# A gated unit whose normalisation and split go batch by batch, in a program whose order comes from another scheduling simulation

## The chip, the cores and the metric

The kernel runs on one core of one Trainium2 chip. The metric is the device time of one execution in microseconds. Five engines have instruction queues of their own: PE (TensorE, matmuls), DVE (VectorE), ACT (ScalarE), POOL (GpSimd) and SP (SyncE, which here issues the DMAs). Each works through its own queue in order, and semaphores tie the queues together; the order inside each queue is fixed when the program is built.

## The reference, cut to what matters

```python
def _attn_ref(q, k, v):                 # each (8, 8, 1152, 64): batch, head, position, head_dim
    q_pool = q.reshape(B, H, S // 2, 2, D).mean(axis=3)          # 576 queries
    scores = np.matmul(q_pool, k.transpose(0, 1, 3, 2)) / np.sqrt(D)
    attn = np.exp(scores - scores.max(-1, keepdims=True))
    attn = attn / (attn.sum(-1, keepdims=True) + 1e-09)
    return np.matmul(attn, v)

def _moe_ref(x, w_in, w_spatial, b_spatial, w_out):   # x: (8, 576, 512)
    h = np.maximum(x @ w_in, 0.0)                      # 512 -> 1024
    u, v = h[..., :512], h[..., 512:]
    mu, var = mean and variance of v over its 512 columns
    v_n = (v - mu) / np.sqrt(var + 1e-06)
    v_s = np.einsum('ts,bsd->btd', w_spatial, v_n) + b_spatial[None, :, None]
    return (u * v_s) @ w_out                           # 512 -> 512
```

So there are 8 batches of 8 heads of attention, and for each batch a gated unit: a projection, a normalisation of its second half over the columns, a mixing over the 576 positions, a gate and a second projection.

## The kernel before, in words

**Attention.** The heads go two at a time, so there are 32 pairs. For pair i, `attention` runs 18 steps (9 blocks of 128 keys, two heads). A step multiplies keys by queries in two matmuls of 512 columns (L506 and L507, float16 high part and low part) into a PSUM bank `pss` (three of them), and ACT takes the exponential (L512). After every second step POOL subtracts the high part of the result from the whole (`split`, L524), which yields the two operands of the multiplication with the values (L428, L432, L435, twelve short matmuls for a step). The last 64 queries of each head are kept apart (L520, L478 to L480). Beside pair i runs `maxima(i + 1)`: 27 products of queries and keys (L342, L333), each reduced on DVE to row maxima (L348) that a transposition (L356, one for each pair) and a DMA bring to where the next pair's scores need them. `prep` brings the keys and queries two pairs ahead, `values_ahead` the values. When a pair's values are complete, `turn_main` transposes them (L457) into `xg`, the gated unit's input.

**Weights.** The weights lie in memory as doubles. `load_weights` reads them in pieces of 128 x 512 and `from_double` (L144) turns each into float32 with six DVE instructions and two on ACT. Twelve pieces: eight of `w_in`, four of `w_out`. This is done beside pairs 0 to 8.

**Gated unit.** Two batches make a unit of 1,152 rows, so there are four units, `gated_unit(0)` to `gated_unit(3)`; unit n can begin when pair 8n + 7 is transposed. Units 0, 1 and 2 run beside the attention of the following pairs, unit 3 has nothing beside it but the end of pair 31. The 1,152 rows are nine tiles of 128: four of the first batch, one (tile 4) that holds the last 64 rows of both, four of the second. A unit has four stages:

1. the second half of the projection, nine tiles of twelve matmuls (L582), with relu (L590) and the statistics of each row (L592, L593). When all nine are done, the reciprocal square roots are made for all nine tiles at once by four Newton steps on DVE (L602 to L614);
2. the first half of the projection, transposed (L646, L656), twelve pieces. After each of the first nine, `normalise(t)` (L616) makes one tile's float16 high and low parts: two DVE instructions of 512 columns (L618, L624) and one on ACT (L623);
3. `spatial(e, fc)`, eight calls: the mixing over positions (L688, L689), the bias and the gate on DVE (L695, L698), the sum of squares on ACT (L700);
4. `split(0)` (L703), which finds one scale for the unit from all eight sums of squares, and makes the high and low parts of the gated values with eight instructions on ACT (L718) and eight on DVE (L719), then nine tiles of twelve matmuls (L731, `products`), a scaled copy and the store.

For the last unit, stage 4 is made in two groups of two column blocks: the first group's products are kept and the second group's are added (L773).

**What sets the order.** Every part is a Python generator, and a `yield` marks where another part may come in. The main loop (L809) steps the attention of a pair and with each step its neighbours at fixed rates; a unit gets one step for every two of the attention (`MOE_RATE`). The program order that results is only a priority: when the program is built, a scheduler runs it on a simulated machine, lets each simulated engine take the ready instruction of the highest priority, and writes down the order in which they were taken. That is each engine's queue. The machine simulated is that of the default scheduler (`TileContext(nc)`, L879).

## Time and profile before

| | us |
|---|---|
| median of 3 runs (lowest, highest) | 1373.64 (1370.13, 1375.04) |
| the profiled execution | 1378.83 |
| its span, first to last instruction | 1377.1 |

| engine | busy us | share of the span | instructions |
|---|---|---|---|
| PE | 1222.1 | 89% | 13,696 matmuls |
| DVE | 967.1 | 70% | 2,068 |
| ACT | 970.6 | 70% | 1,632 |
| POOL | 847.0 | 62% | 492 |

The profile's page gives sums over the whole program; the program has stages with different neighbours. What an engine does in a stretch is read from the view of windows (busy microseconds of each engine between two times, with the number of instructions in brackets and the granted TensorE clock), one instruction after another from the timeline. A matmul's duration overlaps that of the next, so PE's busy time says when PE had anything in flight, and not how much more it could have taken; for that the distance from one matmul's start to the next is to be read.

### The profile page before, as it was taken

The page shows a single profiled execution, that of the slowest core. Times are in us where ns is not written, and L with a number is a line of the kernel's source. Part 1 is how long each engine was busy: PE and PEld are TensorE (multiplying, and loading weights), DVE is VectorE, ACT ScalarE, POOL GpSimd, SP SyncE. Part 2 cuts the span into 40 slices and gives each one's busy share as a digit, 9 for nine tenths or more (in the row PEclk, how much of TensorE's full clock was granted, in tenths as well). Part 3 has the DMA queues.
Part 4 walks back from the last instruction along what each step waited for, and adds up shares of the span by engine and source line. Part 5 has one row for each costly group of instructions (what it writes and reads, how often), then busy time and mean ns, then how long its engine had stood idle before and what let it go on. Part 6 is the DMA issues. An engine that isn't in the chain of part 4 may idle for free.

```text
span 1377.1 us, 33478 instructions
## 1 busy us (share of the span) xinstructions
PE 1222.1 (89%) x13696; PEld 741.5 (54%) x13696; DVE 967.1 (70%) x2068; ACT 970.6 (70%) x1632; POOL 847.0 (62%) x492
## 2 busy tenths in 40 slices
PE   3677887788998999889998999889998999899998
PEld 1354555555554665556555666555555566556443
DVE  5799889986869767765668766775667866761455
ACT  6777678779966777768776886768776776655333
POOL 3587677878755666657774766667666576655000
PEclk9998899989999999999999999999999999999999
DMA  7533343434333231244332132244331131101002
GB/s 252 166 97 109 94 124 94 128 93 139 113 96 96 79 94 56 62 126 135 96 96 87 51 91 84 74 118 135 104 96 42 47 94 55 28 24 40 8 1 69
DMA packets 56346, 123.77 MB, mean 90 GB/s; under 512 B 8256, under 2 KB 16448, under 8 KB 56192
## 3 DMA queue, kind: packets, MB, share of 16 engines
q1 hardware_dynamic: 56192, 121.63, 29.8%
q8 instruction: 107, 1.75, 0.5%
q14 instruction: 47, 0.39, 0.1%
HBM read 83.56 MB, written 9.44 MB: 68 GB/s over the span
## 4 chain that ended last, share of the span: by engine, by line
PE 47%; DVE 25%; ACT 8%; POOL 7%; DMA 7%; issue 4%; SPq 1%; POOLq 0%; ACTq 0%; DVEq 0%
DVE mt L348 7%; PE pss L507 5%; PE pss L506 5%; PE pw L688 5%; POOL pt L524 4%; PE pm L342 4%; PE pw L731 4%; PE pw L646 3%; PE o L435 3%; PE o L428 3%; PE pw L582 3%; ACT pt L512 3%; DMA kq<-in_qT_dram 3%; PE o L432 3%; DVE vv L138 2%
## 5 line engine op out<-in xcount | busy, mean ns | idle before, releaser
L524 POOL TENSOR_TENSOR pt<-pt 128x1024 f16<-128x1024 f32 x288 | 567.8, 1977 | 265.9 <-ACT pt L512 253.8
L512 ACT ACTIVATE pt<-pss,lnp,esc 128x512 f32<-128x512 f32 x576 | 439.4, 776 | 156.7 <-PE pss L507 148.1
L348 DVE TENSOR_REDUCE mt<-pm 128x1 f32<-128x384 f32 x730 | 395.8, 552 | 139.1 <-PE pm L342 119.2
L435 PE MATMUL o<-vp,pt 128*128 128x65 f16 x2304 | 282.8, 198 | 20.2 <-POOL pt L524 19.9
L428 PE MATMUL o<-vp,pt 128*128 128x65 f16 x2304 | 284.8, 196 | 13.0 <-DVE xm L443 12.8
L506 PE MATMUL pss<-qhi,khi 128*128 128x64 f16 (+1 forms) x1152 | 279.6, 294 | 9.1 <-ACT pt L512 8.0
L432 PE MATMUL o<-vp,pt 128*128 128x64 f16 x2304 | 284.5, 196 | 0.0
L507 PE MATMUL pss<-xq,klo 66*128 66x64 f16 (+1 forms) x1152 | 280.6, 295 | 4.1 <-DMA xq<-mr 4.1
L428 PEld LDWEIGHTS <-pt 128*128 128x128 bf16 x2304 | 222.7, 101 | 85.1 <-DVE xm L443 22.0
L432 PEld LDWEIGHTS <-pt 128*128 128x128 bf16 x2304 | 221.6, 100 | 50.7 <-issue 10.5
L342 PE MATMUL pm<-khi,qhi 128*128 128x384 f16 x652 | 217.9, 335 | 32.6 <-DVE mt L348 27.7
L435 PEld LDWEIGHTS <-pt 128*128 128x128 f16 x2304 | 220.7, 100 | 31.6 <-POOL pt L524 24.8
L507 PEld LDWEIGHTS <-klo 66*128 66x128 f16 x1152 | 99.1, 100 | 48.8 <-issue 17.3
L132 ACT ACTIVATE klo<-kq 128x1152 f16<-128x1152 f32 x64 | 74.6, 1166 | 63.7 <-DMA kq<-in_kT_dram 49.4
L506 PEld LDWEIGHTS <-khi 128*128 128x128 f16 x1152 | 103.5, 100 | 27.9 <-issue 12.2
L342 PEld LDWEIGHTS <-qhi 128*128 128x128 f16 x768 | 76.8, 101 | 66.3 <-issue 28.5
L524 POOL TENSOR_TENSOR ptl<-ptl 128x1152 f16<-128x1152 f32 x32 | 71.1, 2221 | 57.9 <-ACT ptl L520 57.9
L305 POOL TENSOR_TENSOR klo<-kq,khi 128x640 f16<-128x640 f32 x64 | 85.1, 1341 | 20.1 <-ACT khi L304 19.8
L520 ACT ACTIVATE ptl<-pss,lnp,esc 128x256 f32<-128x256 f32 (+1 forms) x128 | 75.6, 591 | 24.8 <-PE pss L507 24.2
L264 POOL TENSOR_TENSOR vp<-vt,vp 128x576 f16<-128x576 f32 x64 | 80.6, 1264 | 20.3 <-ACT vp L262 20.3
L582 PE MATMUL pw<-wi_h,xg 128*128 128x512 f16 x240 | 90.1, 382 | 0.0
L731 PE MATMUL pw<-wo_h,vv 128*128 128x512 f16 x216 | 80.3, 381 | 4.7 <-DVE vv L138 4.7
(177 smaller groups left out, 2394.2 us busy)
## 6 DMA issues: line engine op xcount, KB each, us to landing
vt<-in_v_dram SPq DMA_DIRECT2D x64, 576.0 KB
kq<-in_kT_dram SPq DMA_DIRECT2D x32, 576.0 KB
kq<-in_qT_dram SPq DMA_DIRECT2D x32, 576.0 KB
khi<-khi SPq DMA_DIRECT2D x96, 144.0 KB
out_dram<-row SPq DMA_DIRECT2D x24, 256.0 KB
qhi<-xq SPq DMA_DIRECT2D x64, 72.0 KB
klo<-klo SPq DMA_DIRECT2D x32, 144.0 KB
vv<-in_w_in_dram SPq DMA_DIRECT2D x8, 512.0 KB
```

The source lines that it names most:

```text
L305: nc.gpsimd.tensor_sub(KL[:, 0, a:z], k0[:, a:z], khh[:, 1, a:z])
L342: nc.tensor.matmul(pm[:, :W], lhsT=qhl[:, h, c0 : c0 + P], rhs=khh[:, h, n * NB : (n + 1) * NB, :], start=True, stop=True,)
L348: nc.vector.reduce_max(out=mt[:, t, n : n + 1], in_=pm[:, :W], axis=AX.X)
L428: nc.tensor.matmul(o[:, t], lhsT=top[:, cols], rhs=vp[:, D : D + D1], start=c == 0 and t == 0, stop=False, skip_group_check=True,)
L432: nc.tensor.matmul(o[:, t, 0:D], lhsT=top[:, cols], rhs=vp[:, 0:D], start=False, stop=False, skip_group_check=True)
L435: nc.tensor.matmul(o[:, t], lhsT=rst[:, cols], rhs=vp[:, D : D + D1], start=False, stop=c == NC - 1, skip_group_check=True,)
L506: nc.tensor.matmul(o, lhsT=khh[:, h, c, :], rhs=qhl[:, h, q], start=True, stop=False)
L507: nc.tensor.matmul(o, lhsT=KL[0:KR, h, c, :], rhs=X[0:KR, h, q], start=False, stop=True)
L512: nc.scalar.activation(pt, ps, AF.Exp, bias=lnp, scale=esc)
L524: nc.gpsimd.tensor_sub(t.bitcast(F16)[:, :, 0::2], t, t.bitcast(BF16)[:, :, 1::2])
L582: nc.tensor.matmul(ph, lhsT=xa[:, cc, c0 : c0 + P], rhs=wa[:, cc, DH:DF], start=n == 0, stop=n == 3 * NCC - 1,)
L731: nc.tensor.matmul(py, lhsT=ga[:, fc, c0 : c0 + P], rhs=wa[:, fc, :], start=m == 0, stop=m == end - 1)
```

## The change

There are three edits. Line numbers in the changed program differ a little: L582 is now L626, L646 is L660, L688 and L689 are L702 and L703, L731 is L749.

1. `from_double` takes the low word as an unsigned number straight from the source, so the shift that made it signed (L151) is gone: five DVE instructions for a piece instead of six.
2. `gated_unit` works by batch. The reciprocal square roots are made twice, for tiles 0 to 4 after tile 4 and for tiles 5 to 8 after tile 8, with three Newton steps instead of four. `normalise` begins in stage 1, after tile 5, and goes on in stage 2 after every second piece. There is one scale for each batch instead of one for each unit (or group): `split(0)` runs beside the spatial stage of the second batch, `split(1)` and `split_tails` beside the products of the first batch's tiles. The parts are written over the normalised tiles that are no longer needed. All four units now go the same way; the last unit's two groups and their final addition are gone.
3. The context is made with `schedule_with_timeline_sim=True`: the scheduler's simulated machine is another one, so the order of every engine's queue is written anew.

```diff
-        V.tensor_scalar(out=t2, in0=lo, scalar1=1, scalar2=None, op0=ALU.logical_shift_right)
-        yield
-        V.scalar_tensor_tensor(out=dst, in0=t2, scalar=2.0 ** -51, in1=dst, op0=ALU.mult, op1=ALU.add)
+        yield
+        V.scalar_tensor_tensor(out=dst, in0=lo, scalar=2.0 ** -52, in1=dst, op0=ALU.mult, op1=ALU.add)
...
+        def deviations(c):
+            v_, s_, r_ = va[:, c], sd[:, c], rs[:, c]
+            nc.vector.tensor_scalar_add(v_, mv[:, c, 1], 1e-6)
...
+            for k in range(3):
+                z = SVN if k == 2 else 1.0
+                nc.vector.tensor_mul(s_, r_, r_)
...
+            if t > 4:
+                normalise(done)
+                done += 1
+            if t in (4, NT - 1):
+                deviations(slice(0, 5) if t == 4 else slice(5, NT))
+            yield
...
-                if done < NT:
+                if done < NT and (3 * fc + i) % 2 == 0:
                     normalise(done)
                     done += 1
...
+        def split(e):
+            s_g, r_g = yield from scale_of(gsq[:, e * NFC : (e + 1) * NFC], "g")
+            s_gs.append(s_g)
+            nc.vector.tensor_mul(r_y[:, e : e + 1], r_g, wsc["wo"])
...
+            m0 = 0 if e == 0 else MAIN + P
+            for fc in range(NFC):
+                x = u[:, fc, m0 : m0 + MAIN]
+                h, l = vh[:, 5 * e + fc, 0:MAIN], vh[:, 5 * e + fc, MAIN : 2 * MAIN]
+                head(h, x, s_g)
+                rest(l, x, s_g, h)
+                yield
+
+        def split_tails():
+            for e in range(2):
+                x = u[:, :, MAIN + e * TAIL : MAIN + (e + 1) * TAIL]
+                head(gte[:, 0, :, e], x, s_gs[e])
+                rest(gte[:, 1, :, e], x, s_gs[e], gte[:, 0, :, e])
+                yield
...
+        def chain(gens):
+            for g in gens:
+                yield from g
+
+        def beside(main, other, every):
+            for n, _ in enumerate(main):
+                if n % every == 0:
+                    other = step(other)
+                yield
+            while other is not None:
+                other = step(other)
+                yield
+
+        yield from chain(spatial(0, fc) for fc in range(NFC))
+        yield from beside(chain(spatial(1, fc) for fc in range(NFC)), split(0), 3)
+        yield from beside(chain(products(t) for t in range(4)), chain([split(1), split_tails()]), 2)
+        yield from chain(products(t) for t in (5, 6, 7, 8, 4))
...
-    with _tile.TileContext(nc) as tc:
+    with _tile.TileContext(nc, schedule_with_timeline_sim=True) as tc:
```

The order changes on every engine and all through the program. Three places show how.

**DVE, after the first pair's maxima.** (`mx`, `mr`, `qks`, `qkr`, `esc` and `qhi` belong to the chain from one pair to the next; `vv` and `u` at L149 to L161 are the pieces of the weights.) Before:

```order
L352 TENSOR_REDUCE mx<-mt 128x9
L149 TENSOR_SCALAR vv<-vv 128x512
L358 TENSOR_SCALAR mr<-pm 9x128
L117 TENSOR_SCALAR qkh<-pm 128x2
L359 SCALAR_TENSOR_TENSOR mr<-pm,mr 9x128
L121 TENSOR_SCALAR qks<-qkh 128x2
L122 TENSOR_SCALAR qkr<-qkh 128x2
L161 TENSOR_TENSOR u<-u,vv 128x512
L287 SCALAR_TENSOR_TENSOR esc<-qkr 128x1
L151 TENSOR_SCALAR vv<-vv 128x512
L138 SCALAR_TENSOR_TENSOR qhi_120<-kq,qks,xq_114 128x576
```

The same place now (L139 is the former L138, L118 to L123 the former L117 to L122):

```order
L352 TENSOR_REDUCE mx<-mt 128x9
L358 TENSOR_SCALAR mr<-pm 9x128
L118 TENSOR_SCALAR qkh<-pm 128x2
L359 SCALAR_TENSOR_TENSOR mr<-pm,mr 9x128
L122 TENSOR_SCALAR qks<-qkh 128x2
L123 TENSOR_SCALAR qkr<-qkh 128x2
L287 SCALAR_TENSOR_TENSOR esc<-qkr 128x1
L159 SCALAR_TENSOR_TENSOR vv<-vv 128x512
L150 TENSOR_SCALAR vv<-vv 128x512
L139 SCALAR_TENSOR_TENSOR qhi_120<-kq,qks,xq_114 128x576
```

The short chain instructions no longer have a piece of the weights between them, but more pieces have gone through by then: of the instructions at L149 to L161, 10 of 72 stood ahead of the 27th maximum and 22 ahead of the 54th; now 15 of 60 and 36.

**PE, unit 1's products.** Before, beside pairs 22 to 24, three matmuls of the unit (L731) stand between two steps of the attention:

```order
L506 LDWEIGHTS khi_118
L506 MATMUL pss<-qhi_121,khi_118 128x512
L507 LDWEIGHTS klo_109
L507 MATMUL pss<-xq_115,klo_109 128x512
L342 LDWEIGHTS qhi_119
L342 MATMUL pm<-khi_116,qhi_119 128x384
L731 LDWEIGHTS vv
L731 MATMUL pw<-wo_h,vv 128x512
L731 LDWEIGHTS vv
L731 MATMUL pw<-wo_l,vv 128x512
L731 LDWEIGHTS vv
L731 MATMUL pw<-wo_h,vv 128x512
```

Now the first products of unit 1 (L749) come in a run, behind a run of attention:

```order
L507 LDWEIGHTS klo_107
L507 MATMUL pss<-xq_113,klo_107 128x64
L749 LDWEIGHTS vv
L749 MATMUL pw<-wo_h,vv 128x512
L749 LDWEIGHTS vv
L749 MATMUL pw<-wo_l,vv 128x512
L749 LDWEIGHTS vv
L749 MATMUL pw<-wo_h,vv 128x512
```

Counted over the whole program in pairs of attention that stand beside a stage in PE's queue, unit 1 had 1.5 pairs beside stage 1, 1.75 beside stage 2, 2.0 beside stage 3 and, 0.45 pairs later, 1.8 beside stage 4. Now it has 0.9, 1.0 and 1.0; then 2.4 pairs with no matmul of a unit, then 1.5 beside stage 4, and 1.1 pairs with none before unit 2 begins. For unit 0 the two empty stretches are 1.6 and 1.1 pairs, for unit 2 the first is 2.2.

**PE, the end of the attention.** Before, the last transposition (L457, L463) stands among unit 2's last products:

```order
L731 LDWEIGHTS vv
L731 MATMUL pw<-wo_l,vv 128x512
L457 MATMUL pm<-ident,xm 128x128 x4
L463 MATMUL pm<-ident_98,xt 128x64 x4
L731 LDWEIGHTS vv
L731 MATMUL pw<-wo_h,vv 128x512
```

Now it stands among unit 3's first projections (L626), and unit 2's products end before pair 31:

```order
L626 LDWEIGHTS xg
L626 MATMUL pss<-wi_l,xg 128x512
L626 LDWEIGHTS xg
L626 MATMUL pss<-wi_h,xg 128x512
L457 MATMUL pm<-ident,xm 128x128 x4
L463 MATMUL pm<-ident_98,xt 128x64 x4
L626 LDWEIGHTS xg
L626 MATMUL pss<-wi_h,xg 128x512
```

Of unit 3's 108 matmuls of stage 1, none stood ahead of the last transposition; now 66 do, those that need only pairs before the last.

153 lines of the change are left out of this document (55 added, 98 removed).

## The prediction

> **What bounds the kernel now.** I read the page's engine sums and chain first, then the windows by pair, then the timeline for PE's true rate.
>
> ```profile
> PE 1222.1 (89%) x13696; PEld 741.5 (54%) x13696; DVE 967.1 (70%) x2068; ACT 970.6 (70%) x1632; POOL 847.0 (62%) x492
> PE 47%; DVE 25%; ACT 8%; POOL 7%; DMA 7%; issue 4%; SPq 1%; POOLq 0%; ACTq 0%; DVEq 0%
> ```
>
> PE looks full at 89%, but the chain that ended last spends only 47% of the span on it and changes hands all the time. How much PE could still take shows in the distance between starts (timeline, PE alone; start, duration):
>
> ```profile
> 1262.62 0.38 PE L731 MATMUL pw<-wo_h,vv 128*128 128x512 f16 x1
> 1262.84 0.38 PE L731 MATMUL pw<-wo_l,vv 128*128 128x512 f16 x1
> 1263.06 0.38 PE L731 MATMUL pw<-wo_h,vv 128*128 128x512 f16 x1
> 1263.27 0.19 PE L428 MATMUL o<-vp,pt 128*128 128x65 f16 x1
> 1263.30 0.19 PE L432 MATMUL o<-vp,pt 128*128 128x64 f16 x1
> 1263.33 0.20 PE L435 MATMUL o<-vp,pt 128*128 128x65 f16 x1
> ```
>
> A matmul of 512 columns takes its turn every 0.216 us, one of 64 every 0.03, whatever their durations say. So one pair of attention costs PE: 36 x 0.216 = 7.8 for the scores, 216 x 0.03 = 6.5 for the values, 27 maxima of 384 columns at 0.162 = 4.4, and some 3.6 for tails and transpositions by the same rates: 22.3 us (an estimate). A unit costs 424 x 0.216 for its wide matmuls and 6 for its narrow ones: 97.6 us. Now the pairs, whose ends are the transpositions at L356, one for each:
>
> ```profile
> L356 PE MATMUL pm<-ident,mx x32: 269/273/383, 38.6 to 1229.3; 128*9 128x128 f32 x32
> ```
>
> The mean is (1229.3 - 38.6) / 31 = 38.4 us a pair. Windows cut at these transpositions (from:to, length, then busy time and count of PE, PEld, DVE, ACT, POOL, then clock and DMA):
>
> ```profile
> 637.00:953.00 316.00, 295.45 (x3422) 180.99 (x3419) 217.53 (x487) 233.40 (x389) 208.42 (x120) 0.98 0.31 92
> 676.00:713.00 37.00, 35.71 (x410) 21.61 (x408) 22.81 (x57) 27.86 (x46) 25.95 (x16) 1.00 0.30 89
> 713.00:760.00 47.00, 40.63 (x423) 23.94 (x421) 35.52 (x87) 30.35 (x51) 28.22 (x16) 0.93 0.24 71
> 760.00:797.00 37.00, 36.38 (x441) 23.18 (x442) 27.53 (x58) 31.52 (x52) 25.57 (x15) 1.00 0.26 74
> 876.00:918.00 42.00, 34.46 (x395) 20.63 (x394) 34.23 (x62) 30.11 (x51) 28.60 (x17) 0.96 0.14 39
> ```
>
> Eight pairs with a unit beside them take 316 us, of which PE needs 8 x 22.3 + 97.6 = 276. An ordinary pair takes 37 us and PE needs 22.3 + 97.6 / 7.7 (the unit is spread over 7.7 pairs) = 35.0, or 94%: there PE is the bound. Two pairs are not ordinary. From 713 to 760 DVE does 87 instructions, the normalisation among them, and PE waits: 10 us more than 37. From 876 to 918 DVE splits the gated values while PE has no unit matmul: 5 us more. So a unit carries 15 us of stalls that bunched DVE work makes. The first eight pairs are another stage:
>
> ```profile
> 120.00:160.00 40.00, 32.00 (x395) 21.19 (x395) 35.44 (x68) 29.25 (x50) 27.83 (x16) 0.87 0.35 97
> 288.00:320.00 32.00, 27.66 (x357) 18.19 (x357) 28.34 (x63) 26.39 (x46) 25.10 (x14) 0.90 0.33 99
> ```
>
> There DVE is busy 35 of 40 us, with maxima and with the weights, and it is the bound. The window from 288 to 320 is one pair with hardly any weights: 32 us, with ACT at 26.4. These two windows price what comes next.
>
> **The change part by part, against the profiled execution's 1378.8 us.**
>
> The shift that goes:
>
> ```profile
> L151 DVE TENSOR_SCALAR vv<-vv 128x512 int32<-128x512 int32 x12 | 14.2, 1184 | 0.1
> ```
>
> 12 x 1184 ns = 14.2 us of DVE, in the stage that DVE bounds: at most -14. Against it stands the order. Ahead of the 54th maximum there were 22 instructions of the weights and now there are 36; 14 more at about 1.18 us put 16 us more in front of the maxima that pair 1's scores wait for, through SP's two DMAs of `mr`. The debt is paid back in pairs 2 to 4, which have 13 fewer, but not below 32 us a pair, so little of it returns. I take 0, between -14 and +16.
>
> The three units. With the normalisation cut in two and begun in stage 1, and both splits laid beside PE's work, the 15 us of stalls should go. What the DVE work costs stays the same (the rows of the two normalising instructions and of two that make up a Newton step):
>
> ```profile
> L618 DVE TENSOR_SCALAR row<-vv,mv,rs 128x512 f32<-128x512 f32 x36 | 32.7, 922 | 0.3
> L624 DVE TENSOR_TENSOR vv<-row,vv 128x512 f16<-128x512 f32 x36 | 35.5, 1008 | 2.5 <-ACT vv L623 2.3
> L613 DVE TENSOR_SCALAR sd<-sd 128x9 f32<-128x9 f32 x16 | 7.5, 468 | 0.3
> L611 DVE TENSOR_TENSOR sd<-rs 128x9 f32<-128x9 f32 x16 | 2.7, 166 | 0.3
> ```
>
> Nine tiles are 17.4 us a unit as before. Two sets of three Newton steps are 8 x 15 - 4 x 19 = 44 small instructions more, at 0.17 to 0.47 us each 2 to 5 us a unit. I cost these at nothing: they stand beside stages 1 and 2, where PE has 35 us of work a pair and DVE 23 to 28; without that cover they cost those 2 to 5. The splits' elements are the same in number.
>
> The new order takes back a part. It pushes a unit's stages together and leaves pairs with no unit matmul: 2.7, 3.5 and 2.2 for units 0, 1 and 2, a mean of 2.8. In such a pair PE has 22.3 us and ACT bounds: 26.4 us of work at the 94% that a full engine reached above is 28; the window with some weights took 32. I take 29, nearer to the first because DVE's weights are gone by then. The other 5.2 pairs hold the whole unit: 5.2 x 22.3 + 97.6 = 213.6 us of PE, at 94% 227. Eight pairs then take 2.8 x 29 + 227 = 308 where 316 stood: -8 a unit, -23 for three. The bounds: 32 us an empty pair and PE at 90% give 90 + 237 = 327, +11 a unit or +33; ACT's bare 27 and PE at 98% give 76 + 218 = 294, -22 a unit or -67.
>
> The last unit:
>
> ```profile
> 1229.00:1266.60 37.60, 37.60 (x467) 23.18 (x466) 4.33 (x17) 24.08 (x35) 22.93 (x12) 1.00 0.14 44
> 1266.60:1377.00 110.40, 105.43 (x664) 51.24 (x660) 53.53 (x123) 37.73 (x71) 1.90 (x1) 1.00 0.08 27
> ```
>
> Of the 110 us after the attention PE needs 97.6. Now 66 matmuls (66 x 0.216 = 14 us) stand ahead of the last transposition, but the pair they stand in has only some 29 - 22 = 7 us of room for them: -7. Against it, `split(1)` begins its chain (the sum, PE's scale, five small DVE instructions, ACT, DVE) with 13 matmuls or 2.8 us of products left in front of those that need it: I add 2. Together -5, between -13 (all 14 us hidden, 1 lost) and +3.
>
> The sum: 0 - 23 - 5 = -28, so 1351 for an execution like the profiled one. That one stands 5.2 us above the median shown (1378.83 against 1373.64), which makes **1346 us** to be compared with 1373.64.
>
> **The rivals.**
>
> *DVE comes too late for the new order (slower).* An order taken from a simulated machine holds when each engine is as fast as that machine thinks. DVE's small instructions are not steady: the Newton row's mean of 468 ns stands against 166 ns for the same-sized ones at L611. And the new queue puts nine normalisations within 0.3 pairs of maxima, where they took 0.55. If DVE falls behind there, PE's queue stands at a maximum or at stage 3 as it does now, the 15 us stay, and the pairs without unit matmuls come on top: 323 a unit, +7, +22 for three; the weights' 16 us in front of the second pair come for the same reason, and the end gains nothing. 1378.8 + 38 - 5 = 1412. It decides from the point where DVE has over 35 us of work a pair, as from 713 to 760. Against it: the stage 2 matmuls now stand where PE used to have only attention to wait with.
>
> *The order fits well (much faster).* PE's waits fall too, not only the stalls:
>
> ```profile
> PE pm L342 <- DVE mt L348: 27.7, 35, 2.2
> PE o L435 <- POOL pt L524: 19.9, 24, 2.3
> ```
>
> These are queue heads that wait while other matmuls are ready, just what another order can change. With the low bounds, -14 - 67 - 13 = -94: 1280. Against it: engines that share work unevenly lose what they gain.
>
> *It comes out even.* If an empty pair takes the 32 us of the window quoted, at PE's 94%, eight pairs take 317 against 316, the stalls' gain is given back exactly, and the early and last terms cancel: 1371 to 1374.
>
> *The clock falls in the empty pairs.* PE's granted clock was 0.93 and 0.96 in the two stalled windows, 0.87 to 0.90 in the first stage, 1.00 in the full pairs. At 0.87 an empty pair's 22.3 us are 26, still under ACT's 28, and nothing changes. At half clock they are 45, 16 us over 29, and 2.8 x 3 pairs cost 131: 1477. [...]
>
> **How the numbers follow.** The forecast has 0.49 (its own range 1325 to 1368), the late DVE 0.23, the good fit 0.14, the even case 0.12, the clock 0.02. What a measurement of this kernel can tell from no change is about 0.5%, 1366.8 to 1380.5. Faster: 0.46 of the forecast's 0.49 and the 0.14, 0.60. Same: the even case and a little of the forecast, 0.15. Slower: 0.25. The range reaches into the good fit and to near the late DVE's 1412, leaving out about half of each and the clock: 1295 to 1405.
>
> **What would show it.** The second and the ninth transposition start now at
>
> ```profile
> L356 PE MATMUL pm<-ident,mx x1: 277/277/277, 73.0 to 73.0; 128*9 128x128 f32 x1
> L356 PE MATMUL pm<-ident,mx x1: 277/277/277, 320.4 to 320.4; 128*9 128x128 f32 x1
> ```
>
> Each step right: no pair in units 0 to 2 with DVE over 35 us and PE waiting; windows of 28 to 30 us where no unit matmul runs, and of over 40 us where stages 1 to 3 do, with PE at 94% of its turn; the second transposition some 5 to 15 us later than 73 and the ninth about where it is; the stretch after the attention near 105 us. Wrong: empty pairs at 32 us or more, PE's waits for DVE at L348 longer than 27.7 us in all, or a first stage that ends later than 330 us. A gap over 5 us before tile 5's products in the last unit would make the end term wrong.

## The result, and the profile after

The changed kernel takes 1447.53 us (median of 4 runs, 1443.95 to 1451.15) where the kernel before takes 1371.89 on the same chip: ratio 1.055, 95% interval 1.0509 to 1.059. It is slower by 76 us; forecast were 28 us less. The profiled execution is the longest of the four (1451.15 us); its span is 1449.4 us.

The page of the changed kernel, its engine sums (busy time, share, instructions):

```profile
PE 1259.5 (87%) x13702; PEld 757.1 (52%) x13702; DVE 957.1 (66%) x2122; ACT 972.9 (67%) x1640; POOL 829.3 (57%) x492
```

Its groups by line, cut to the pairs' transpositions: first to last, then the second and the ninth alone (start of the first and the last):

```profile
L356 PE MATMUL pm<-ident,mx x32: 270/277/372, 41.1 to 1321.8; 128*9 128x128 f32 x32
L356 PE MATMUL pm<-ident,mx x1: 278/278/278, 83.3 to 83.3; 128*9 128x128 f32 x1
L356 PE MATMUL pm<-ident,mx x1: 273/273/273, 334.6 to 334.6; 128*9 128x128 f32 x1
```

No engine has more work worth the name: DVE has 10 us less (957.1 after 967.1), ACT 2 us more. PE's busy time is 37 us longer although it has only six matmuls more. A pair takes (1321.8 - 41.1) / 31 = 41.3 us where it took 38.4. The eight pairs of unit 1, cut at the transpositions (from:to, length, busy time and count of PE, PEld, DVE, ACT, POOL, then clock, DMA share, GB/s):

```profile
678.00:740.00 62.00, 53.01 (x519) 30.95 (x518) 42.52 (x105) 35.86 (x62) 27.93 (x17) 0.89 0.25 73
740.00:788.00 48.00, 47.05 (x522) 28.62 (x520) 26.95 (x58) 32.76 (x59) 26.65 (x16) 1.00 0.24 69
788.00:841.50 53.50, 50.85 (x553) 28.90 (x551) 37.36 (x77) 28.26 (x50) 22.96 (x13) 1.00 0.21 62
841.50:874.00 32.50, 26.75 (x285) 16.38 (x286) 23.59 (x52) 24.92 (x39) 21.76 (x13) 0.84 0.23 65
874.00:909.30 35.30, 28.44 (x342) 19.31 (x342) 22.79 (x47) 26.05 (x46) 27.27 (x17) 0.85 0.43 127
909.30:950.00 40.70, 36.72 (x476) 23.07 (x472) 26.52 (x57) 31.82 (x53) 27.74 (x17) 1.00 0.36 108
950.00:990.40 40.40, 38.73 (x414) 22.81 (x414) 23.77 (x56) 28.65 (x46) 23.67 (x14) 0.96 0.39 114
990.40:1022.00 31.60, 28.76 (x338) 17.47 (x338) 24.76 (x57) 25.16 (x42) 25.91 (x16) 1.00 0.29 86
```

Together 344 us where 316 stood. The order does what the rows said: three crowded pairs, then two with no unit matmul, then the products. But the crowded ones take 163.5 us, and the first of them, with 105 DVE instructions in it, 62. The two pairs without unit matmuls take 32.5 and 35.3, at a mean clock of 0.84 and 0.85; the last, with 19 matmuls of unit 2 in it, takes 31.6. The other stages: pairs 0 to 7, then the last pair after its transposition, and the end behind the attention:

```profile
41.10:334.60 293.50, 231.87 (x2756) 147.79 (x2757) 220.84 (x454) 220.80 (x369) 205.98 (x118) 0.89 0.38 113
1321.80:1358.50 36.70, 32.91 (x375) 20.39 (x375) 6.79 (x23) 17.83 (x26) 18.90 (x10) 0.91 0.01 2
1358.50:1449.40 90.90, 86.27 (x533) 41.98 (x531) 42.20 (x118) 34.18 (x67) 0.00 (x0) 1.00 0.08 27
```

Stage by stage, from the starts of the same transpositions in each trace (pairs 0 to 7 from the span's start; the column "end" runs from the 32nd to the end), with the later kernels of this study:

```
                 to 9th  pairs 8-15  16-23  24-30   end    span
before            320.4     317.2    316.2  275.5  147.7  1377.1
after             334.6     343.7    343.7  299.8  127.6  1449.4
default_order     312.3     328.1    320.1  282.9  144.1  1387.4
norm_late         311.8     320.9    318.5  278.6  144.0  1373.7
shift_three       309.2     314.3    317.6  274.0  147.8  1363.0
before_new_order  338.6     343.3    347.0  295.2  128.8  1452.9
act_held          334.8     341.7    327.4  290.2  133.6  1427.7
```

So the change costs 14 us in the first stage and 24 to 28 with each unit, and gains 20 at the end. PE's longest waits after it (total us, times, longest):

```profile
PE pm L342 <- DVE mt L348: 36.5, 45, 3.7
PE pss L506 <- ACT pt L512: 22.8, 29, 2.6
PE pm L356 <- DVE mx L352: 16.1, 13, 5.4
PE pss L507 <- DMA xq<-mr: 15.6, 17, 3.4
```

Before, the first was 27.7 and the third 13.4; the other two have grown most:

```profile
PE pss L506 <- ACT pt L512: 8.0, 9, 4.5
PE pss L507 <- DMA xq<-mr: 4.1, 1, 4.1
```

One wait is gone: PE's for `pt` from GpSimd at L435, 19.9 us before, is 1.2 us now. No single wait explains 72 us. The experiments take the change apart first, then the order.

### The profile page after: what moved, and what is told of

The parts are those of the page before. It is cut to its first block, busy times and chain, and to the rows that moved or that the text cites. A ratio compares the mean times of both kernels' runs of the same rounds, so it can differ in the third digit from the quotient of the medians.

```text
span 1449.4 us, 33579 instructions
## 1 busy us (share of the span) xinstructions
PE 1259.5 (87%) x13702; PEld 757.1 (52%) x13702; DVE 957.1 (66%) x2122; ACT 972.9 (67%) x1640; POOL 829.3 (57%) x492
## 3 DMA queue, kind: packets, MB, share of 16 engines
q8 instruction: 107, 1.75, 0.5%
## 4 chain that ended last, share of the span: by engine, by line
PE 36%; DVE 8%; DMA 4%; ACT 2%; issue 1%; POOL 0%; SPq 0%; ACTq 0%; DVEq 0%; POOLq 0%
PE pss L507 4%; PE pss L506 4%; PE pw L702 4%; PE pw L749 4%; PE pw L660 3%; DVE mt L348 3%; PE pm L342 3%; PE pw L626 2%; PE o L435 2%; PE o L428 2%; PE o L432 2%; PE pss L702 1%; DMA xq<-mr 1%; PE pss L626 1%; PE pss L749 1%
## 5 line engine op out<-in xcount | busy, mean ns | idle before, releaser
L524 POOL TENSOR_TENSOR pt<-pt 128x1024 f16<-128x1024 f32 x288 | 553.6, 1932 | 355.7 <-ACT pt L512 333.1
L512 ACT ACTIVATE pt<-pss,lnp,esc 128x512 f32<-128x512 f32 x576 | 429.2, 777 | 167.3 <-PE pss L507 112.0
L348 DVE TENSOR_REDUCE mt<-pm 128x1 f32<-128x384 f32 x720 | 384.6, 551 | 205.2 <-PE pm L342 153.2
L506 PE MATMUL pss<-qhi,khi 128*128 128x64 f16 (+1 forms) x1152 | 289.1, 303 | 30.0 <-ACT pt L512 22.8
L507 PE MATMUL pss<-xq,klo 66*128 66x64 f16 (+1 forms) x1152 | 284.3, 304 | 15.6 <-DMA xq<-mr 15.6
L428 PE MATMUL o<-vp,pt 128*128 128x65 f16 x2304 | 280.3, 198 | 6.7 <-DVE xm L443 6.6
L432 PE MATMUL o<-vp,pt 128*128 128x64 f16 x2304 | 279.1, 197 | 0.0
L435 PE MATMUL o<-vp,pt 128*128 128x65 f16 x2304 | 273.3, 199 | 1.2 <-POOL pt L524 1.2
L428 PEld LDWEIGHTS <-pt 128*128 128x128 bf16 x2304 | 224.4, 102 | 59.0 <-issue 17.8
L342 PE MATMUL pm<-khi,qhi 128*128 128x384 f16 x642 | 207.3, 342 | 41.2 <-DVE mt L348 36.5
L435 PEld LDWEIGHTS <-pt 128*128 128x128 f16 x2304 | 224.1, 101 | 31.6 <-issue 13.4
L507 PEld LDWEIGHTS <-klo 66*128 66x128 f16 x1152 | 103.1, 103 | 94.6 <-issue 53.5
L506 PEld LDWEIGHTS <-khi 128*128 128x128 f16 x1152 | 108.1, 104 | 66.8 <-issue 38.1
L342 PEld LDWEIGHTS <-qhi 128*128 128x128 f16 x768 | 73.7, 102 | 87.8 <-issue 51.9
L348 DVE TENSOR_REDUCE mt<-pw 128x1 f32<-128x384 f32 x144 | 75.9, 547 | 18.7 <-PE pw L342 12.2
L660 PE MATMUL pw<-xg,wi_h 128*128 128x512 f16 (+1 forms) x336 | 80.4, 328 | 1.7 <-ACT u L670 1.7
## 6 DMA issues: line engine op xcount, KB each, us to landing
khi<-khi SPq DMA_DIRECT2D x96, 144.0 KB
klo<-klo SPq DMA_DIRECT2D x32, 144.0 KB
```

Source lines behind the costliest of these rows:

```text
L342: nc.tensor.matmul(pm[:, :W], lhsT=qhl[:, h, c0 : c0 + P], rhs=khh[:, h, n * NB : (n + 1) * NB, :], start=True, stop=True,)
L348: nc.vector.reduce_max(out=mt[:, t, n : n + 1], in_=pm[:, :W], axis=AX.X)
L428: nc.tensor.matmul(o[:, t], lhsT=top[:, cols], rhs=vp[:, D : D + D1], start=c == 0 and t == 0, stop=False, skip_group_check=True,)
L432: nc.tensor.matmul(o[:, t, 0:D], lhsT=top[:, cols], rhs=vp[:, 0:D], start=False, stop=False, skip_group_check=True)
L435: nc.tensor.matmul(o[:, t], lhsT=rst[:, cols], rhs=vp[:, D : D + D1], start=False, stop=c == NC - 1, skip_group_check=True,)
L506: nc.tensor.matmul(o, lhsT=khh[:, h, c, :], rhs=qhl[:, h, q], start=True, stop=False)
```

## Experiments: the parts of the change

Ratios are to the kernel before, measured beside each run. Three kernels separate the order, the shift and the unit.

**default_order**: the changed kernel without the new order.

```diff
-    with _tile.TileContext(nc, schedule_with_timeline_sim=True) as tc:
+    with _tile.TileContext(nc) as tc:
```

> The changed kernel with its order from the default scheduler again: the decoding without the shift and the unit by batch stay. Theory 'the order' (the new simulated machine's order costs the time, the two other edits gain): 1330 to 1350 us, ratio 0.97 to 0.985, with eight pairs beside a unit at about 305 instead of 344 and the first eight pairs at 308 to 320 instead of 335. Theory 'the unit' (the normalisation and split by batch make the stages collide, the order only follows): 1420 to 1450, and eight pairs beside a unit stay at 335 or more.

Measured: 1390.72 us, ratio 1.0118 (1.0091 to 1.0145). Both expectations miss; it lies between.

**before_new_order**: the kernel before, with the new order alone (the same line the other way).

> The kernel before with nothing changed but the scheduler's simulated machine. Theory 'the order': 1440 to 1480 us, ratio 1.05 to 1.08, the first eight pairs at 335 or later, eight pairs beside a unit at 340 or more. Theory 'the unit': 1365 to 1385, ratio 0.995 to 1.01.

Measured: 1458.31 us, ratio 1.0615 (1.0571 to 1.0659), as 'the order' expected.

**shift_only**: the kernel before with the new `from_double` alone.

```diff
-        lo, hi = src[:, 0::2], src[:, 1::2]
+        lo, hi = src.bitcast(U32)[:, 0::2], src[:, 1::2]
...
-        V.tensor_scalar(out=t2, in0=lo, scalar1=1, scalar2=None, op0=ALU.logical_shift_right)
```

> The kernel before with only the shift of the decoding taken out (12 DVE instructions of 1184 ns), default scheduler. If DVE bounds the first eight pairs and the order keeps its shape, 10 to 14 us of the 14.2 come off: 1358 to 1364, ratio 0.990 to 0.993, the ninth transposition at 307 to 311 instead of 320. If the first stage is bound elsewhere, within 3 us of before.

Measured: 1367.46 us, ratio 0.9943 (0.9912 to 0.9974): a gain of some 8 us, less than the 10 to 14 expected, and its ninth transposition starts at 309.3 instead of 320.4. The 14 us of DVE that go are worth 11 at the end of their stage.

So the new order costs 1447.5 - 1390.7 = 57 us on the changed kernel and 1458.3 - 1374.8 (the kernel before, measured beside it) = 83 on the one before, and the unit's part costs 1390.7 - 1367.5 = 23 instead of gaining. Where those 23 are, the windows of default_order show: the pairs with the normalisations (two), the one after them, and two around the first split:

```profile
675.60:721.40 45.80, 40.43 (x414) 23.31 (x413) 36.23 (x81) 34.07 (x56) 28.07 (x17) 0.93 0.30 88
721.40:763.90 42.50, 38.26 (x421) 22.92 (x422) 37.47 (x83) 29.70 (x50) 27.25 (x15) 0.96 0.27 78
763.90:800.00 36.10, 36.10 (x443) 23.27 (x442) 19.71 (x50) 28.32 (x49) 24.82 (x16) 1.00 0.26 75
...
839.10:882.70 43.60, 39.80 (x468) 23.51 (x467) 35.53 (x74) 30.55 (x53) 28.07 (x17) 1.00 0.26 76
882.70:924.00 41.30, 36.43 (x419) 22.32 (x418) 30.48 (x65) 27.91 (x48) 23.20 (x14) 1.00 0.34 99
```

and its longest wait of PE (total us, times, longest):

```profile
PE pm L342 <- DVE mt L348: 54.5, 61, 3.7
```

Before, one pair had 87 DVE instructions and took 47 us, between two of 37. Now two pairs in a row have 81 and 83 and take 45.8 and 42.5: one stall of 10 us over 37 has become two, of 9 and 5. The first split, laid beside mixing, makes another pair with DVE busy 35.5 us, 43.6 long, and the pair after it still takes 41.3. In the two pairs and in the one at the split DVE has over 35 us, and PE's wait for the maxima's buffers has doubled from 27.7 to 54.5 us.

**norm_late**: default_order, with the deviations taken once for nine tiles and the normalisation left in stage 2 as before; the split by batch and three Newton steps stay.

```diff
-            if t > 4:
-                normalise(done)
-                done += 1
-            if t in (4, NT - 1):
-                deviations(slice(0, 5) if t == 4 else slice(5, NT))
+            if t == NT - 1:
+                deviations(slice(0, NT))
...
-                if done < NT and (3 * fc + i) % 2 == 0:
+                if done < NT:
```

> The changed kernel in the default order (1391 us), with the reciprocal square roots again made once for nine tiles (three steps) and the normalisations only in stage 2, one for each of the first nine pieces. The split by batch stays. Theory 'normalisation in stage 1' (it falls where DVE has the statistics too, and PE's maxima wait): 1376 to 1384, the two slow pairs there (45 and 47 us) become one. Theory 'the split beside the mixing': 1388 to 1394, and the slow pair at the mixing (44 us) stays.

Measured: 1375.7 us (10 runs), ratio 1.0035 (1.0011 to 1.0059), at the fast edge of the first expectation; the slow pair at the mixing, which the second expected to stay, stays too. Its windows have the old form at the normalisation and the new one at the split:

```profile
668.30:705.90 37.60, 36.49 (x413) 22.02 (x412) 22.94 (x57) 28.71 (x48) 25.77 (x15) 1.00 0.35 101
705.90:752.60 46.70, 38.18 (x422) 22.41 (x420) 38.06 (x84) 32.29 (x54) 28.26 (x16) 1.00 0.25 74
827.80:871.50 43.70, 39.73 (x467) 23.50 (x466) 35.64 (x74) 30.55 (x54) 28.17 (x17) 1.00 0.25 76
871.50:914.70 43.20, 38.02 (x420) 22.88 (x419) 30.97 (x65) 28.06 (x48) 23.24 (x14) 0.96 0.33 94
```

**shift_three**: shift_only with three Newton steps where four stood.

```diff
-        for k in range(4):
-            z = SVN if k == 3 else 1.0
+        for k in range(3):
+            z = SVN if k == 2 else 1.0
```

> The kernel before without the shift (1367.5 us) and with three Newton steps where four stood, nothing else, old order. A step is one instruction of 468 ns, three of 166 ns: 1.0 us at each of four units, 4 us in all. If these lie on the path, as the stall of 10 us at the normalisation says: 1362 to 1365 us. If other work of VectorE or the next wait takes their place: 1366 to 1369 us, no difference that can be told.

Measured: 1363.63 us, ratio 0.9927 (0.9901 to 0.9954): the fastest kernel of the study, faster than both. Whether the step itself counts cannot be told from shift_only's 0.9943. It differs from norm_late by what comes with the split by batch alone (the last unit's single way included). The two pairs at the split, in unit 1, it has as

```profile
823.10:861.70 38.60, 38.12 (x465) 23.12 (x464) 27.42 (x64) 25.28 (x45) 24.91 (x15) 1.00 0.30 85
861.70:905.50 43.80, 34.04 (x400) 20.72 (x399) 35.41 (x66) 32.28 (x54) 29.46 (x17) 1.00 0.16 40
```

38.6 + 43.8 = 82.4 against 43.7 + 43.2 = 86.9: these two pairs are 4.5 us longer, and the pair that the split left hardly gets shorter. By the table above most of that comes back within unit 1 (318.5 against 317.6 for its eight pairs); in the other two units the difference is 6.6 and 4.6 us, and the end is 3.8 us shorter. The longer way at the split is thus seen in the windows, its price only in the sum of 1.1%.

**dev_three** and **te_act** ask why the unit's part costs anything, since the large instructions are the same. In default_order the small ones are not. Its groups by line (busy us, mean ns), the second copy of the edge tile and the first product of a Newton step:

```profile
L616 DVE COPY te<-vv 64x512 f16<-64x512 f16 x4 | 6.0, 1489 | 0.1
L597 DVE TENSOR_TENSOR sd<-rs 128x5 f32<-128x5 f32 (+1 forms) x24 | 9.5, 396 | 0.5
```

The same copy in the groups of before (the product, L611, is in the prediction with 166 ns):

```profile
L628 DVE COPY te<-vv 64x512 f16<-64x512 f16 x4 | 1.2, 288 | 0.1
```

The timeline of default_order at such copies (start, duration):

```profile
399.13 3.84 POOL L524 TENSOR_TENSOR pt<-pt 128x1024 f16<-128x1024 f32 x2
399.33 1.89 DVE L616 COPY te<-vv 64x512 f16<-64x512 f16 x1
401.23 1.89 DVE L617 COPY te<-vv 64x512 f16<-64x512 f16 x1
```

Two copies of 0.29 us that start beside a GpSimd instruction last 1.89 us each; the second ends at 403.12, 0.15 us behind the end of the GpSimd row at 402.97. Of the 136 small instructions (deviations and copies) of default_order 29 last over 0.35 us, 1.52 in the mean; the other 107 last 0.17. Before, there were 92, and 7 of them long. In both kernels the last unit, which has hardly any GpSimd work beside it (1.9 us behind 1266.6 in before), has no long one (0.29 us at most in before). In the traces of before and after, 25 of 228 small instructions start beside a GpSimd instruction; 22 of these last over 0.35 us, and each of the 22 ends 0.02 to 0.15 us behind the end of a GpSimd instruction. None of the other 203 lasts over 0.35 us.

This accounts for the two pairs at the normalisation: in default_order VectorE has 36.2 + 37.5 = 73.7 us in them, in norm_late 22.9 + 38.1 = 61.0, and the small instructions there take 18.9 and 6.2 us, which is the whole difference of 12.7.

dev_three is norm_late with three times the small instructions at the same place:

```diff
             if t == NT - 1:
-                deviations(slice(0, NT))
+                for k in range(0, NT, 3):
+                    deviations(slice(k, k + 3))
```

> norm_late (1375.7 us) with the deviations taken in three calls of three tiles, one behind the other at the same place, where one call took nine: 30 small VectorE instructions more in each unit, nothing else. In default_order two calls of them and the four edge copies cost 11.2 + 4.3 = 15.5 us of VectorE a unit where they cost 5.1 + 1.5 = 6.6 before; the same instruction has 0.17 to 0.28 us where GpSimd is idle and some 1.5 us where it starts beside one of GpSimd's, 25 times of 88 there, 7 of 64 before. Theory 'small instructions, each at the risk of a wait for GpSimd, lie on the path': 30 x 0.3 to 0.45 us = 9 to 13 us a unit for four units, 1395 to 1430 us. Rival 'their place counts, not their number' (the stall there is long anyway): 1374 to 1381 us.

Measured: 1419.22 us, ratio 1.032 (1.028 to 1.036): 43 us more than norm_late for 120 small instructions, 0.36 us each. In its trace the deviations take 52.2 us of VectorE (17.8 in norm_late), and the copies behind them, now beside GpSimd, 18.2 (4.6): 48 us more, 34 of them in 23 more long ones. In units 0 to 2 these instructions take 43 us more, and pairs 8 to 30 are 42 us longer, so there such time is on the path. In the last unit they take 5 us more, none of them is long, and the end is 144.0 us in both.

te_act is default_order with the copies on ScalarE:

```diff
-                nc.vector.tensor_copy(out=te[0:TAIL, 0, :], in_=h[0:TAIL])
+                nc.scalar.activation(te[0:TAIL, 0, :], h[0:TAIL], AF.Copy, bias=0.0, scale=1.0)
```

> default_order (1390.7 us) with the four edge copies of the normalisation done by ScalarE instead of VectorE. They cost VectorE 17.2 us in all there and 5.9 before (1489, 1169, 1088 and 531 ns each, 284 to 632 before). Theory 'VectorE's time in its crowded pairs is on the path, and part of it is the wait for GpSimd': 3 to 4 us a unit in three units go, 1378 to 1383 us. Rival 'hidden, or ScalarE's queue pays the same': 1387 to 1395 us.

Measured: 1391.8 us, ratio 1.0126 (1.0088 to 1.0164): nothing gained, as the rival expected, although the copies' 17 us of VectorE are gone. So the number and place of the small instructions costs, but not each of them; the copies' 4 us a unit are off the path there or are paid on ScalarE, which is busy 10.5 us longer.

Taken in this order of steps the ratios add up, each step with some 0.4% of uncertainty: the shift and the Newton step -0.7%, the split by batch 1.0035 - 0.9927 = +1.1%, the early normalisation with its second set of deviations 1.0118 - 1.0035 = +0.8%, the new order 1.055 - 1.0118 = +4.3%; in all 5.5%. The second set is 60 small instructions, which at dev_three's 0.36 us would be 21 us, more than the 0.8% (some 11 to 15 us), so what the earlier place costs by itself is not measured. The parts are not independent either: with the order first it is +6.2% for the order, and the other edits then gain 0.7%.

## Experiments: what the order costs

A function of the scheduler's context, called `keep` below, pins an instruction behind everything already written for its engine. With it one set of instructions is put back into the order of the program, while the new order makes the rest. (Where `keep` is in a kernel, its line numbers are one higher.)

**unit_held**: the units' matmuls pinned, so that they spread over the pairs again.

```diff
+    keep = tc.keep_in_program_order
...
-                    nc.tensor.matmul(
+                    keep(nc.tensor.matmul(
```

> The changed kernel with the new order, but each matmul of a unit on PE must stand behind everything that the program wrote for PE before it, so a unit's stages spread over eight pairs again (1.4, 1.8, 2.0 and 1.8 pairs, nearly no empty pairs). Theory 'bunching' (a unit drawn together starves the attention in three pairs and PE in the next two): eight pairs beside a unit fall from 344 to 320 to 328, the stretch after the attention goes back from 91 to 104; in sum 1385 to 1410. Theory 'the attention's own order' (runs of scores and runs of values, whatever the unit does): 335 or more for eight pairs, 1430 or more in sum.

Measured: 1468.02 us, ratio 1.0705 (1.0657 to 1.0754). The rival's range holds. The units are spread, every pair of pairs 8 to 30 has unit matmuls, and eight pairs still take 342 and 344 us. With the bunching gone nothing is gained, unless the pin has a price that hides it.

**pe_held**: all matmuls and transpositions pinned, in the same way.

> The changed kernel with the new order for DVE, ACT, POOL and SP, but every matmul and transposition on PE in the order the program wrote it. If PE's order is what costs: 1380 to 1400 (the default order gave 1391), the first eight pairs at 312 to 320. If the other engines' queues cost: 1415 or more, the first eight pairs still at 330 or later.

Measured: 1528.49 us, ratio 1.1162 (1.1118 to 1.1205). PE in the program's order beside four queues in another is worse than all five in the new one.

**decode_held**: the weights' DVE instructions in `from_double` pinned.

> The changed kernel with the new order, but each of the weights' DVE instructions (60 of them) must stand behind everything that the program wrote for DVE before it. Theory 'weights ahead of the maxima': the second transposition goes from 83 back to 72 and the ninth from 335 to 315 to 322, in sum 1425 to 1437. Theory 'the attention's own order': the ninth stays at 330 or later, 1440 or more.

Measured: 1468.15 us, ratio 1.0711 (1.0661 to 1.0761). The second transposition comes at 75.2, near the 73.0 of before, and the ninth at 337.6 all the same. So the weights' instructions up front are not what makes it long, again unless the pin has a price of its own.

**act_held**, **sp_held** and **paps_held**: ScalarE's queue, SyncE's, and all but VectorE's pinned, each instruction wrapped in `keep` as above.

> The changed kernel under the new order, with ScalarE's instructions alone kept in the order in which the program writes them; all other queues as the new order makes them. Theory 'ScalarE's queue': in the changed kernel GpSimd waits 333.1 us for ACT's pt (253.8 before) and PE's L506 waits 22.8 us for ACT's pt (8.0 before), because the new order mixes weights, norms and exponentials differently. Put back, ScalarE would give 1385 to 1425 us and GpSimd's wait for ACT would fall below 280 us. Rival 'one queue against the rest': an order holds only if all engines follow it, and a queue put back alone is out of step with the others, as it was when PE was put back alone (1528.5): 1445 us or more, and GpSimd's wait for ACT above 300 us.

Measured: 1429.46 us, ratio 1.0413 (1.0378 to 1.0448): 18 us less, and GpSimd's wait down to 253.2. The wait is as the first theory expected; the time lies between the two ranges, 4 us above the first.

> The changed kernel under the new order, with the DMA issues of SyncE alone kept in the order of the program. Theory 'the transfers': PE's waits for DMAs at L507 and L342 grew from 4.1 + 10.4 us to 15.6 + 15.4 us; with the issues put back these 16 us and what hangs on them go, 1420 to 1435 us. Rival 'one queue against the rest': 1445 us or more. If the transfers' order is only a symptom, within 5 us of 1447.5 with the same two waits at about 30 us in all.

Measured: 1577.53 us, ratio 1.1467 (1.1419 to 1.1515), 130 us worse than with the new order; PE's wait at L508 (L507 before) for `xq` from `mr` is 68.2 us.

> The changed kernel under the new order, with four queues (PE, ScalarE, GpSimd and SyncE) kept in the order of the program; only VectorE still follows the new order. Theory 'one queue against the rest' in its mild form: what costs is that queues depart from the order of the program, so with four of five put back it gives 1385 to 1415 us, near the 1390.7 of the old order, and far below the 1528.5 of PE alone. Theory 'VectorE's queue': VectorE's maxima and conversions in the new order are what the others wait for; then it stays at 1440 us or more. Third: the order of the program is itself a bad one for these queues, and the old order was not the program's: above 1500 us.

Measured: 1610.93 us, ratio 1.1729 (1.1692 to 1.1765). The third expectation holds: the order of the program is a bad one for these queues, and the old order, at 1390.7, was not that order. A queue that gets slower when pinned therefore says nothing against the new order of that queue; only a gain is telling. VectorE's whole queue was not tried in the order of the program.

**before_act_held** repeats the one edit that gained on the other kernel, and **actpool_held** adds GpSimd's queue.

> The kernel before under the new order (1458.3 us), with ScalarE's instructions alone kept in the order of the program. The same edit took 18 us from the changed kernel. Theory 'ScalarE's queue carries a third of the order's price': it takes as much here, 1432 to 1446 us, and GpSimd's wait for ACT's pt falls from 323.8 to below 270 us. Rival 'each edit makes another order, and the time scatters': the wait may fall, but the time lies anywhere from 1440 to 1475 us; above 1450 speaks for it.

Measured: 1432.42 us, ratio 1.0443 (1.0402 to 1.0484): 26 us less than before_new_order. GpSimd's row among the waits of the changed kernel

```profile
POOL pt L524 <- ACT pt L512: 333.1, 124, 18.2
```

and of act_held:

```profile
POOL pt L525 <- ACT pt L513: 253.2, 118, 8.5
```

The same row of before_new_order

```profile
POOL pt L524 <- ACT pt L512: 323.8, 121, 17.7
```

and of before_act_held:

```profile
POOL pt L525 <- ACT pt L513: 262.3, 114, 8.1
```

On both kernels the pin takes 61 to 80 us from GpSimd's wait for exponentials, halves the longest, and gains 18 and 26 us. So ScalarE's queue carries about a third of the order's price. By the table above the gain lies in pairs 16 to 30 (343.7 to 327.4 and 299.8 to 290.2); the first sixteen pairs keep their length, and the end gives back 6 us.

> The changed kernel under the new order, with ScalarE's and GpSimd's instructions both kept in the order of the program (ScalarE's alone gave 1429.5 us). Theory 'a departure costs on each queue by itself': another gain, 1405 to 1425 us. Rival 'the order of the program helps on ScalarE alone': 1427 to 1435 us, no further change. Third, as with SyncE's queue, the order of the program is a bad one for GpSimd: above 1440 us.

Measured: 1441.66 us (1434.61 to 1446.43), ratio 1.0504 (1.044 to 1.0569): no gain over act_held, and not clearly a loss. GpSimd's queue carries none of it that this can show.

**The clock.** The window rows of after show 0.84, 0.85 and 0.89. Taken apart, these are not clocks but mixtures of half and full. Windows of 3.41 us around 858 (length, PE, PEld, DVE, ACT, POOL, clock):

```profile
854.90:858.30 3.40, 2.79 (x28) 1.47 (x25) 3.37 (x5) 3.21 (x6) 3.40 (x3) 1.00 0.09 22
858.30:861.74 3.44, 1.34 (x18) 0.72 (x16) 3.36 (x5) 3.44 (x7) 3.02 (x3) 1.00 0.19 43
861.74:865.15 3.41, 3.41 (x30) 2.13 (x27) 1.56 (x3) 1.37 (x3) 3.41 (x4) 0.50 0.48 109
865.15:868.57 3.42, 3.27 (x46) 2.07 (x47) 3.07 (x11) 3.42 (x6) 2.80 (x2) 1.00 0.03 7
```

PE is busy 39% of the second window, and in the third its clock is exactly half, while it has work all the time. The timeline of PE in after, ten us earlier at full clock, and in the third window (start, duration):

```profile
852.81 0.38 PE L506 MATMUL pss<-qhi,khi 128*128 128x512 f16 x1
853.03 0.38 PE L507 MATMUL pss<-xq,klo 66*128 66x512 f16 x1
...
863.97 0.63 PE L506 MATMUL pss<-qhi,khi 128*128 128x512 f16 x1
864.40 0.63 PE L507 MATMUL pss<-xq,klo 66*128 66x512 f16 x1
```

The distance between the two is 0.22 us at full clock and 0.43 at half. PE's whole time from 38 us on can be divided by such distances: a matmul's own turn (the tenth percentile of its line and size), what a turn begun at half clock is longer, up to double, and the remaining gaps:

```
                  longer at half clock   gaps   granted half
before                    33.7 us       239.4      91.6 us
default_order             32.7          248.5      82.8
after                     59.5          278.9     156.1
act_held                  55.3          261.4     136.6
shift_three               25.3          233.0      64.5
```

Here the last column is the sum of the records at half. From default_order to after the turns at half clock grow by 26.8 us and the gaps by 30.4, 57 together: the order's price on this kernel, nearly half of it in matmuls that run at half clock. On the kernel before it is otherwise: from before to before_new_order, 76 us longer by their spans, the same division has 33.7 and 43.0 us at half clock, 9 more, and 61 us more of gaps (an estimate from the two traces). What the order brings on both is the gaps. That is a division of PE's time; whether the clock's share would be gained if only the clock stayed up, three runs were to tell. They issue the first score matmul of each tile twice in pairs where PE has gaps. A tile has two matmuls, high and low part, and only one of them is doubled: 18 a pair, and not the 36 that the expectations count. So fill_first has 144 more (13,840 after 13,696), 31 us at 0.216 instead of 62; fill_more has 54 beyond that (12 us), fill_after 216 (47 us), and the filler covers less of the gaps than was meant.

```diff
+            if i < 8:
+                nc.tensor.matmul(ps, lhsT=khh[:, h, c, :], rhs=qhl[:, h, MAINS[h]], start=True, stop=True)
             products(ps, c, h, MAINS[h])
```

> The kernel shift_three (1363.6 us) with the first score matmul of each 512-column tile issued twice in the first eight pairs: 8 x 36 matmuls of 0.216 us, 62 us of needless PE work where PE had 106 us of gaps; the second issue overwrites the first, so the result is the same. It tells whether the granted clock costs anything by itself: the clock records of shift_three are halves and wholes only, and 37.5 us of its first eight pairs lie at half. Theory 'the clock is on the path': the stretches at half clock in the first stage fall below 12 us, and up to 13 us go: 1350 to 1359 us. Rival 'other engines bind there, the clock only follows': the half clock goes all the same, and the time stays within 3 us, 1360.5 to 1366.5. Third 'the filler stands in the way': 1370 us or more.

Measured, in the third expectation's range: 1385.08 us, ratio 1.009 (1.0064 to 1.0117), and 53 us at half clock between the first and the ninth transposition instead of 37.5.

> As fill_first, with the same filler in three more pairs, those during which the unit splits its gated values and has no matmuls (attention 14, 22 and 30, with 9 to 13 us of PE gaps each); 23 us more of needless PE work. They hold 10 us at half clock in shift_three. Theory 'the clock is on the path': 1 to 5 us less than fill_first. Rival 'the clock only follows': the same as fill_first within 2 us. Third: 3 to 8 us more, where the filler goes in front of what other engines wait for.

Measured: 1398.17 us, ratio 1.019 (1.0162 to 1.0217), another 13 us, beyond the third expectation.

> The changed kernel under the new order (1447.5 us), with the first score matmul of each 512-column tile issued twice in the twelve pairs that have few or no unit matmuls there (attention 0 to 6, 12, 19, 20, 27, 28): 12 x 36 x 0.216 = 93 us of needless PE work; the order is made anew with them in it. The changed kernel has 156 us at half clock, the kernel before 92. Theory 'the clock is on the path': half clock below 90 us, and 15 to 30 us go: 1417 to 1433 us. Rival 'the clock only follows the waits': 1440 to 1455 us. Third 'the filler stands in the way': 1465 us or more.

Measured, the third again: 1473.88 us, ratio 1.0737 (1.0709 to 1.0765), with 153 us at half clock (156 in after). The first stage of shift_three and of fill_first, by windows,

```profile
38.90:309.20 270.30, 212.46 (x2715) 139.01 (x2715) 235.06 (x450) 217.82 (x368) 209.53 (x117) 0.93 0.38 115
38.80:326.20 287.40, 234.25 (x2849) 150.23 (x2849) 226.46 (x448) 221.82 (x372) 209.22 (x119) 0.91 0.38 112
```

and of fill_after:

```profile
42.40:317.90 275.50, 230.60 (x2853) 147.19 (x2854) 209.91 (x449) 217.30 (x364) 201.84 (x115) 0.94 0.40 118
```

In the old order the filler makes the stage 17 us longer (309.2 to 326.2 at the ninth transposition); that it stands ahead of what others wait for, with the gaps elsewhere, is a reading and not shown. In the new order, made anew with it, the same stage becomes 17 us shorter (334.6 to 317.9) and the later ones longer. In that one stage half clock did fall, from 64.9 to 35.6 us, which is what the clock theory asks for; but the order of every queue changed with it, so the gain cannot be put down to the clock. Over whole kernels the half clock was not taken away, so its price by itself stays unmeasured; for the longer turns alone the bounds are 0 and the 26.8 us above.

## Why the prediction was wrong

The measured 1447.53 us is beyond the range and on the other side; the forecast's sign had 0.60, the slower side 0.25.

**"With the normalisation cut in two ... the 15 us of stalls should go"** failed, and this without any new order: in default_order the unit's part costs 23 us instead of gaining. The step took a stall for a matter of where the work stands beside PE's. The windows show a matter of how much DVE has in a pair: in place of one such pair at the normalisation there are two with DVE over 36 us (45.8 and 42.5 us long), and the split moved beside mixing made a third. The large instructions are the same; what the two pairs have more of is the small ones. So **"I cost these at nothing"** is the term under it: the small instructions of a unit, deviations and copies, took 6.6 us of DVE before and 15.6 in default_order, 9 more where 2 to 5 were allowed for, because in their new places more of them meet a GpSimd instruction and wait it out (29 last over 0.35 us where 7 did). dev_three shows that such time of the deviations is on the path in units 0 to 2; for the copies' share, 3 of the 9 us, it is not shown, since te_act gained nothing by taking them away. In place of -15 a unit, the early normalisation with its second set of deviations cost 0.8% and the split by batch 1.1%. The late rival's sentence, that DVE decides from 35 us a pair, fits these rows, and those of the order of before as well.

**"29 us an empty pair, 94% in the others: 308"** was mis-sized on both sides. Pairs with no unit matmul took 32.5 and 35.3 us (unit 1), and the one before unit 2 gets going 31.6, not 29; the forecast called 32 the sign of a wrong step. The three crowded pairs took 163.5 us, and their matmuls' own turns sum to some 135, or 83%. In all 344 instead of 308. But bunching, to which the step put the order's price down, was not shown to be its cause: spread again, a unit costs as much, though there the pin may have a price of its own. About a third is ScalarE's queue, on both kernels. The rest, some 40 us, most of it in the first sixteen pairs, is not settled: no pin took it away, and why the order costs it stays open.

**"I take 0" for the first stage** failed. The second transposition came 10 us later, within the forecast 5 to 15; the debt was then not paid back, and the ninth came 14 us later, near the upper bound of +16. Yet its reason, the weights up front, fell as well: with them put back the ninth still came at 337.6 (decode_held). What is right is the shift's worth: 11 us at the ninth transposition, of 14 at most.

**"Together -5" for the last unit** had the right sign and was too small: 20 us less from the 32nd transposition on, and 91 us behind the attention, not 105. But the gain is not free: pairs 24 to 30, which take 24 us more, now hold 577 of the units' matmuls where they held 525, since unit 2's products end there. These 52, of 512 columns each, are 11 us of turns.

**The clock rival** reckoned with "0.87 to 0.90 in the first stage" as if a mean were a clock. That is a wrong reading: the 94 records of before and after know 0.5 and 1 alone, in periods of 3.41 us and multiples but for the last record of each, and 0.87 over 40 us is half clock for 10 us of them. Nor was 0.87 the least: the 40 us from 132 to 172 of the kernel before have 0.79. And half clock came without an empty window: it followed one with PE busy 39% at 861.74 us of after. The 0.02 was the author's estimate. The rival's form, whole pairs at half clock for 131 us, did not come, but half clock went from 92 to 156 us and, by the division above, bears up to 27 of the order's 57 us here, and 9 of 76 on the kernel before.

**The signs** named beforehand did their work: L348's wait above 27.7 us (36.5), a first stage ending later than 330 (334.6), two empty pairs of unit 1 over 32.

## What to carry to other kernels

Work that stalls a pipeline is not made harmless by cutting it in two: ask in how many stages the helping engine then has more than it can do, and price each of them, the small instructions by what runs beside them at the new place. An order computed from a model is a change to every queue at once, so measure it apart from the edit it comes with; here it was three quarters of the loss, or more than all of it when it is taken first. Read a mean clock between a half and one as a share of time at half clock, where the records know 0.5 and 1 alone as these do; here half clock came behind a window whose longest gap was 2.10 us (after, at 861.74 us).

## What was not expected of the hardware

In the traces of before and after there are 47 windows of 3.41 us at full clock followed by half clock. PE was busy 41% of them in the median and never over 67%; 42 windows as thin as that were not followed by a drop. The 45 returns to full clock all came behind a window in which PE was busy 82% or more. PE's longest gap in the window ahead of the drop at 861.74 us of after was 2.10 us. In these two traces half clock therefore follows thin windows, not only empty ones. Time at half clock mostly rises with the span: 64.5 us at 1363 (shift_three), 91.6 at 1377 (before), 156.1 at 1449 (after), 277.9 at 1577 (sp_held) and 309.9 at 1610 (paps_held). It does not rank the kernels, though: before_new_order has 121.4 us at 1453, and actpool_held has 35 us less than act_held (101.2 and 136.6) with no shorter time. This is no proof that the half clock costs the time.

In default_order a VectorE copy of 0.29 us took up to 1.89 us beside a GpSimd instruction, and a Newton product of 0.17 us up to 1.85: the mean of a small instruction (468 ns against 166 in the forecast's rows) is a mixture as well, of a free and a blocked one.
